# A new order table and a new choice of engines for the same operations: attention, a dense layer and a routed layer in one kernel

## The chip, the cores and the metric

The kernel runs on one core of one Trainium2 chip. The metric is the device time of one execution, in microseconds (us). The engines are named as in the profile: PE is TensorE (matmuls and transposes; PEld is its loading of weights), DVE is VectorE, ACT is ScalarE, POOL is GpSimd, SP is SyncE, which issues most DMAs.

## The reference, cut to what matters

```python
# attention: q, k, v are (2, 8, 768, 64); keys within 16 of the query, and 24 pooled blocks of 32
k_sum, v_sum = blocks of k (max) and of v (mean)
scores_l = where(|i - j| < 16, scale * q @ k.T, -1e9)
scores_s = scale * q @ k_sum.T + log(32)
a = softmax over both, with + 1e-09 in the divisor
x = (a @ [v, v_sum]) as 1536 tokens x 512
# dense layer (d_ff 768)
h = maximum(maximum(x @ w1, x @ w2), x @ w3);  x = h @ w_out
# routed layer: 8 experts, F = 1024
do_compute = x @ w_skip > 0;  logits = x @ w_gate;  e = argmax(logits);  g = its softmax weight
out = x;  out[do_compute] = x + g * (maximum(x @ w1[e], 0) @ w2[e])
```

## The kernel before, in words

**Stages.** The first stage is attention, for 4 groups of 384 tokens and 4 pairs of heads: scores (PE, L226 and L231), masked row maximum (DVE, L243), exponent (ACT, L250), divisor (DVE, L255 and L256), scaling (POOL, `norm`, L260), transposes (PE, L265) and their copies (L270), the product with the values (PE, L278). Its result is split into a high part and a low part (`xh` L286, `xl` L289), whose products are summed to keep fp32 accuracy. The dense layer's weights lie in memory as 64-bit words and are converted on the chip in steps (L305 to L330, on ACT, POOL and DVE), which also give a high and a low part. A chain (L337) is 12 matmuls of one group, one block of the hidden layer and one of the three weights; L344 (ACT) and L346 (DVE) take the maximum, L351 and L354 split the result, L364 multiplies by `w_out`, and L370 to L388 copy the sums out, from where DMAs write them to `out` and to `x2d`. A fold (L402 to L427) multiplies `w_out` with the gate and the skip weights, so that the logits come out of the same matmuls.

**Routing.** For each group `route` (L467 to L493) finds the experts, `rp` (PE, L509 to L512, with the counts L542) the place of each token among those of its expert, `rd` (`route3`, DVE, L521 to L531) the row, and three indirect DMAs on POOL (`rs`, L536) write token numbers and gate weights to `table`. The three of one group follow one another: each waits for the one ahead of it to land.

**The second layer.** It goes by pairs of tiles of 128 tokens of one expert. The tokens of a pair are gathered from `x2d` by the rows of `table` (`fetch`, POOL, L718, into `xn`), transposed (`turn_x`, PE, L705) and split into high and low (`put_x`, ACT L712 into `xth`, DVE L713 into `xtl`). In `pair`, first(f) (L1093) is 12 matmuls for one of 8 blocks of the hidden layer, second(f) (L1105) is 6. At f = 5 the transposes of the next pair stand in PE's queue, so they need the next pair's `xn` by then:

```python
first(0); first(1)
for f in range(8):
    if f == 5:
        turn_x()
    if f + 2 < 8:
        first(f + 2)
    if f == 5:
        next_x(t + 2)
    second(f)
```

 The weights of an expert come as 16 chunks `raw0` to `raw15` (L730), each split into a high part on ACT (`wh`, L736) and a low part on DVE (`wl`, L738). first(0) to first(3) need the chunks 0, 2, 4 and 6, first(4) to first(7) the chunks 1, 3, 5 and 7, second(f) the chunk 8 + f. The names `wl0_2`, `wl1_4` and so on are storage of first-layer weights that is used again.

**Order.** The work up to the first pair is 979 numbered operations. The list `ORDER` (L64 on) gives their numbers in the order in which they are emitted. Each engine works through its own instructions in that order and waits at the first whose inputs or buffers are not ready, so the list sets what stands behind what on each engine. The dictionary `HOME` (L53) names the engine of some operations by kind and index: `c4` (L326, the high part of a weight), `fv` (the copy of the extended values), `ph` (L286), `td` (L270); what is not named there goes to ACT. `w_cb` (L313), `h_low` (L354) and `norm` (L260) call POOL in the code and do not look into `HOME`.

Of the kernel before, what the change touches and what calls it, by code (L numbers as in the profile page):

```python
# [50 lines left out]
PORTED, SWITCH = 0.5, 0.06  # L51

HOME = {  # L53
# [4 lines left out]
}  # L58
HOME = {(n, i): e for (n, e), v in HOME.items() for i in v}

ORDER = [
# [46 lines left out]
]  # L108


# [1300 lines left out]
```

## Time and profile before

| | |
|---|---|
| time, median of 3 runs | 448.0 us (446.93 to 448.46) |
| the profiled execution's own time | 448.98 us |
| its span in the trace | 447.2 us |
| mean granted clock of PE | 0.996 |
| busy: PE, PEld | 432.3 us (97%), 389.2 us (87%) |
| busy: DVE, ACT, POOL | 233.1 us (52%), 184.3 us (41%), 138.1 us (31%) |
| start of the first matmul of the first pair (L1093) | 287.00 us |

A time in a row is counted from the span's start. A row of the timeline joins instructions of one kind that follow one another on one engine (xN of them); what stands in brackets is the time in which the engine was idle ahead of it, and what that wait ended with. An engine's busy share over the whole span says little here, since the stages differ; the windows give it by stretch.

### The profile page before, as it was taken

The numbers are of one execution on the slowest core, as the hardware profiler recorded it, in microseconds if no ns is written. First come the engines' busy times: TensorE is split into PE (matmuls) and PEld (weight loads), VectorE is DVE, ScalarE is ACT, GpSimd is POOL, SyncE is SP. The second block draws the span as 40 slices with busy tenths as digits, with TensorE's granted clock in tenths as the row PEclk, the third lists the DMA queues.
The fourth block names the chain that finished last, engine by engine and source line by source line (L and its number), as shares of the span: only waits on it lengthen the run. The fifth ranks groups of instructions, "written<-read, shape, count | busy, mean of one in ns | idle before, by whom it ended". The sixth has DMA issues, their size and how long they took to land.

```text
span 447.2 us, 9609 instructions
## 1 busy us (share of the span) xinstructions
PE 432.3 (97%) x3558; PEld 389.2 (87%) x3558; DVE 233.1 (52%) x738; ACT 184.3 (41%) x507; POOL 138.1 (31%) x191
## 2 busy tenths in 40 slices
PE   8999999999999999999999999799999999999995
PEld 3668889999789999998999999798989889798874
DVE  4899998989852531043214235868226651232321
ACT  3798984743685754107121037211114521212210
POOL 0666561434222522011601322131316034140400
PEclk9999999999999999999999999989999999999999
DMA  8987556456434512003042390242852193010111
GB/s 281 270 304 247 185 169 221 162 178 200 153 131 128 161 42 75 2 0 122 2 113 77 94 331 1 78 65 49 269 203 94 49 301 128 25 52 2 47 49 32
DMA packets 27584, 56.91 MB, mean 127 GB/s; under 512 B 6099, under 2 KB 8659, under 8 KB 27528
## 3 DMA queue, kind: packets, MB, share of 16 engines
q1 hardware_dynamic: 24968, 50.24, 35.3%
q0 software_dynamic: 2560, 5.96, 4.3%
q8 instruction: 30, 0.49, 0.5%
q14 instruction: 26, 0.21, 0.2%
HBM read 46.69 MB, written 10.47 MB: 128 GB/s over the span
## 4 chain that ended last, share of the span: by engine, by line
PE 83%; DVE 9%; ACT 3%; issue 2%; POOL 2%; DVEq 0%; ACTq 0%; POOLq 0%
PE pm L337 30%; PE ph L1093 13%; PE pm L1105 12%; PE pm L364 11%; PE ph L1186 2%; PE po L278 2%; DVE cx L318 2%; PE sc L226 2%; ACT pr L250 1%; PE pm L159 1%; PE pm L1158 1%; PE pt L265 1%; PE pm L1228 1%; DVE pr L243 1%; POOL pr L260 1%
## 5 line engine op out<-in xcount | busy, mean ns | idle before, releaser
L337 PE MATMUL pm<-xh,wh 128*128 128x384 f32 x288 | 65.2, 346 | 1.2 <-ACT t L344 0.7
L337 PE MATMUL pm<-xl,wh 128*128 128x384 f32 x288 | 62.2, 336 | 0.0
L337 PE MATMUL pm<-xh,wl 128*128 128x384 f32 x288 | 62.2, 335 | 0.0
L1096 ACT ACTIVATE hth<-ph 128x256 fp32r<-128x256 f32 x40 | 15.4, 384 | 91.4 <-PE ph L1093 84.8
L337 PEld LDWEIGHTS pm<-xh,wh 128*128 128x128 f32 x288 | 49.6, 188 | 3.5 <-ACT t L344 1.0
L337 PEld LDWEIGHTS pm<-xl,wh 128*128 128x128 f32 x288 | 51.1, 188 | 0.0
L337 PEld LDWEIGHTS pm<-xh,wl 128*128 128x128 f32 x288 | 51.1, 188 | 0.0
L1097 DVE SCALAR_TENSOR_TENSOR htl<-ph,hth 128x256 fp32r<-128x256 f32 x40 | 16.8, 422 | 56.3 <-ACT hth L1096 56.3
L346 DVE TENSOR_TENSOR t<-pm,t 128x384 f32<-128x384 f32 x48 | 26.1, 553 | 34.7 <-PE pm L337 34.5
L364 PE MATMUL pm<-wh,h 128*128 128x260 f32 (+1 forms) x288 | 43.5, 289 | 0.3 <-ACT x L386 0.3
L260 POOL TENSOR_TENSOR pr<-pr,se 128x360 f32<-128x360 f32 x32 | 27.0, 854 | 50.8 <-DVE se L256 33.1
L250 ACT ACTIVATE pr<-pr,mx 128x120 f32<-128x120 f32 x96 | 36.7, 386 | 12.5 <-DVE mx L243 12.3
L364 PEld LDWEIGHTS pm<-wh,h 128*128 128x128 f32 x288 | 38.2, 190 | 1.6 <-ACT x L386 0.5
L354 POOL TENSOR_TENSOR h<-t,h 128x384 fp32r<-128x384 f32 x24 | 25.3, 1069 | 32.5 <-ACT h L351 32.5
L1105 PE MATMUL pm<-wh,hth 128*128 128x512 f32 x80 | 31.9, 398 | 0.0
L1105 PE MATMUL pm<-wh,htl 128*128 128x512 f32 x80 | 31.6, 395 | 0.0
L1105 PE MATMUL pm<-wl,hth 128*128 128x512 f32 x80 | 31.3, 391 | 0.0
L718 POOL DMA_INDIRECT xn<-x2d,inx x14 | 14.9, 1063 | 48.6 <-DVE xm L1059 29.3
L243 DVE CUSTOM_DVE_ANT_0 pr<-sc,mask 128x120 f32<-128x120 f32 x96 | 21.1, 277 | 16.2 <-PE sc L226 14.1
L344 ACT COPY t<-pm 128x384 f32<-128x384 f32 x24 | 11.4, 478 | 39.9 <-PE pm L337 34.7
L1093 PE MATMUL ph<-xth,wl 128*128 128x256 f32 x160 | 26.2, 285 | 1.5 <-DVE wl L738 1.5
L1093 PE MATMUL ph<-xth,wh 128*128 128x256 f32 x160 | 26.6, 289 | 0.7 <-ACT xth L712 0.7
(337 smaller groups left out, 834.7 us busy)
## 6 DMA issues: line engine op xcount, KB each, us to landing
raw<-in_m SPq DMA_DIRECT2D x48, 256.0 KB, 5.0
raw<-in_wx SPq DMA_DIRECT2D x22, 512.0 KB, 4.3
vx<-in_vx SPq DMA_DIRECT2D x14, 288.0 KB, 3.5
qt<-in_qt SPq DMA_DIRECT2D x16, 192.0 KB, 4.1
raw<-in_vt SPq DMA_DIRECT2D x8, 384.0 KB, 5.9
x2d<-raw SPq DMA_DIRECT2D x12, 256.0 KB, 4.1
kx<-in_kx SPq DMA_DIRECT2D x8, 360.0 KB, 3.7
out<-raw SPq DMA_DIRECT2D x9, 256.0 KB, 3.2
```

The lines of the kernel that those rows point to most:

```text
L243: nc.vector.tensor_tensor_reduce(pr[:, t, :], sc[:, t, :], mask[:, mv, :], -0.125, 3.0e38, ALU.add, ALU.min, mx[:, t:t + 1])
L250: nc.scalar.activation(pr[:, t, :], pr[:, t, :], AF.Exp, bias=mx[:, t:t + 1], scale=-1.0, accum_out=se[:, h, t:t + 1])
L260: nc.gpsimd.tensor_tensor(pr, pr, ST["se", u, p][:, h].unsqueeze(2).broadcast_to([P, TPG, KT]), ALU.mult)
L337: nc.tensor.matmul(ST["ch", u, f, j], l[j, f][:, c * P:(c + 1) * P], r[u][:, c, :], start=(cs[0] == 0 and n == 0), stop=(cs[-1] == KC1 - 1 ...
L346: nc.vector.tensor_tensor(ST["t1", u, f], ps, ST["t1", u, f], ALU.max)
L354: nc.gpsimd.tensor_tensor(HL[u, f], ST["t1", u, f], HH[u, f].bitcast(F32), ALU.subtract)
L364: nc.tensor.matmul(ps, l[u, f][:, t * P:(t + 1) * P], r[3, f][:, lo:hi], start=(part != 1 and n == 0), stop=(part != 0 and n == len(ops) - 1))
L718: nc.gpsimd.indirect_dma_start(out=xn[t], out_offset=None, in_=x2d, in_offset=bass.IndirectOffsetOnAxis(ap=inx[:, t, 0:1], axis=0), bounds ...
L1093: nc.tensor.matmul(ps, w[:, o:o + P], r[:, d, :], start=(n == 0), stop=(n == 3 * KC1 - 1))
L1096: nc.scalar.activation(hh, ps, AF.Relu)
L1097: nc.vector.scalar_tensor_tensor(hl, ps, 0.0, hh.bitcast(F32), ALU.max, ALU.subtract)
L1105: nc.tensor.matmul(py[i], l[:, o:o + P], r, start=(f == 0 and n == 0), stop=(f == 7 and n == 2))
```

## The change

Only two tables differ. `HOME` names other indices: `c4` on POOL goes from 11 to 8 of them, `fv` on POOL from 3 to 6, `ph` on DVE from 4 to 6, `td` on DVE from 3 to 10; and it has entries for `nm`, `hl` and `cb` on DVE. `ORDER` is a new permutation of the same 979 numbers. All code behind the tables is the same and stands 6 lines further down, so L738 of before is L744 of after, L1093 is L1099.

```diff
 HOME = {
-    ("c4", "Pool"): [0, 1, 3, 6, 7, 8, 12, 19, 20, 22, 23],
-    ("fv", "Pool"): [(0, 0), (0, 1), (1, 2)],
-    ("ph", "DVE"): [(0, 0), (0, 2), (1, 1), (1, 2)],
-    ("td", "DVE"): [(0, 0, 1), (0, 2, 1), (1, 3, 1)],
+    ("c4", "Pool"): [0, 1, 2, 5, 6, 19, 20, 22],
+    ("cb", "DVE"): [6, 11],
+    ("fv", "Pool"): [(0, 1), (1, 2), (1, 3), (2, 0), (2, 3), (3, 0)],
+    ("hl", "DVE"): [(0, 0), (0, 2), (0, 3), (0, 4), (1, 0), (1, 1), (2, 0), (2, 3), (2, 4), (2, 5), (3, 0),
+        (3, 1), (3, 2), (3, 3), (3, 5)],
+    ("nm", "DVE"): [(0, 3, 0), (1, 1, 0), (1, 3, 0), (2, 0, 1), (2, 1, 0), (2, 2, 0), (2, 3, 0), (3, 0, 1),
+        (3, 1, 0), (3, 1, 1), (3, 2, 1), (3, 3, 0)],
+    ("ph", "DVE"): [(0, 0), (0, 2), (1, 1), (2, 1), (2, 2), (2, 3)],
+    ("td", "DVE"): [(0, 0, 0), (0, 1, 1), (2, 0, 0), (2, 0, 1), (2, 1, 0), (2, 2, 0), (3, 1, 0), (3, 2, 0),
+        (3, 2, 1), (3, 3, 0)],
 }
...
 ORDER = [
-    5, 25, 27, 6, 49, 26, 7, 0, 51, 50, 8, 28, 34, 52, 35, 9, 37, 36, 10, 73, 29, 11, 38, 12, 76, 58, 39,
...
```

**The end of the first layer on DVE.** `rw`, `rsl`, `rdo` and `rsi` belong to `rd` of the last group, `xm` is a copy of the gathered tokens, `xtl` the low part of the first pair's tokens, `wl` a low part of the second layer's weights. Before, DVE's queue at the end of the first layer reads:

```order
L1059 COPY xm0_3992<-xn0_3476 128x512
L521 TENSOR_TENSOR rw_3790<-pm_3870,con_103 128x24
L1059 COPY xm1_3993<-xn1_3477 128x512
L522 TENSOR_TENSOR rw_3790<-rw_3790,roh_3795 128x24
L524 TENSOR_REDUCE rsl_3890<-rw_3790 128x3
L525 TENSOR_SCALAR rdo_3797<-rdo_3797 128x3
L527 TENSOR_TENSOR rsi_3893<-rsl_3890,rdo_3797 128x3
L531 COPY rw_3790<-pm_3867 1x16
L738 TENSOR_TENSOR wl1_4_3762<-raw13_3465,wh1_4_3761 128x512
L713 TENSOR_TENSOR xtl_3481<-ptx0_3474,xth_3480 128x4x128
L713 TENSOR_TENSOR xtl_3481<-ptx1_3475,xth_3480 128x4x128
L738 TENSOR_TENSOR wl2_3_3727<-raw11_3463,wh2_3_3726 128x512
```

Behind these stand the low parts of the chunks 6, 3, 9 and 1, in this order, and then the first pair's own work. After, the same place reads:

```order
L744 TENSOR_TENSOR wl2_4_3795<-raw14_3465,wh2_4_3794 128x512
L1065 COPY xm0_3992<-xn0_3475 128x512
L1065 COPY xm1_3993<-xn1_3476 128x512
L719 TENSOR_TENSOR xtl_3480<-ptx0_3473,xth_3479 128x4x128
L719 TENSOR_TENSOR xtl_3480<-ptx1_3474,xth_3479 128x4x128
L527 TENSOR_TENSOR rw_3802<-pm_3884,con_103 128x24
L528 TENSOR_TENSOR rw_3802<-rw_3802,roh_3807 128x24
L530 TENSOR_REDUCE rsl_3900<-rw_3802 128x3
L531 TENSOR_SCALAR rdo_3809<-rdo_3809 128x3
L533 TENSOR_TENSOR rsi_3903<-rsl_3900,rdo_3809 128x3
L537 COPY rw_3802<-pm_3881 1x16
L744 TENSOR_TENSOR wl0_5_3798<-raw15_3466,wh0_5_3797 128x512
```

All low parts but that of chunk 15 now stand ahead of `xtl`, and `rd` of the last group has moved from ahead of `xtl` to behind it.

**The low parts that the first pair needs.** Ahead of the last group's `route`, where before had the low parts of the chunks 5, 7, 2, 8 and 4 between the copies of the logits (`lg`), DVE's queue after reads:

```order
L744 TENSOR_TENSOR wl1_1_3608<-raw4_3455,wh1_1_3607 128x512
L744 TENSOR_TENSOR wl1_2_3671<-raw7_3458,wh1_2_3670 128x512
L744 TENSOR_TENSOR wl2_2_3676<-raw8_3459,wh2_2_3675 128x512
L744 TENSOR_TENSOR wl1_0_3577<-raw1_3452,wh1_0_3576 128x512
L744 TENSOR_TENSOR wl2_0_3585<-raw2_3453,wh2_0_3584 128x512
L744 TENSOR_TENSOR wl1_3_3703<-raw10_3461,wh1_3_3702 128x512
L383 COPY lg_3761<-pm_3679 128x9
L744 TENSOR_TENSOR wl0_2_3653<-raw6_3457,wh0_2_3652 128x512
L383 COPY lg_3761<-pm_3706 128x9
```

The low part of chunk 6 has moved from behind `xtl` to ahead of the last group's routing.

**A fold on ACT.** L407 copies transposed `w_out` (`cr`) out of a PSUM buffer in the fold. L250 is the exponent of one tile of scores, three to a head (`pr0`, `pr1`). Before, ACT's queue at the third of the fold's six blocks reads:

```order
L250 ACTIVATE pr0_1719,se_1723<-pr0_1719,mx0_1720 128x120 x3
L407 COPY cr_1774<-pm_1738 128x512
L424 CAST wh3_4_1636<-pm_1728 128x10
L424 CAST wh3_3_1605<-pm_1699 128x10
L305 ACTIVATE cr_1778<-raw_1652 128x512
L250 ACTIVATE pr1_1721,se_1723<-pr1_1721,mx1_1722 128x120 x3
```

After:

```order
L256 ACTIVATE pr0_1711,se_1715<-pr0_1711,mx0_1712 128x120 x3
L430 CAST wh3_3_1568<-pm_1720 128x10
L430 CAST wh3_4_1589<-pm_1728 128x10
L256 ACTIVATE pr1_1713,se_1715<-pr1_1713,mx1_1714 128x120 x3
L413 COPY cr_1798<-pm_1739 128x512
L311 ACTIVATE cr_1805<-raw_1671 128x512
```

The copy has moved behind the exponents of the second head.

## Rows read from the trace of the kernel before

**Rows 1.** The page, part 1: busy time of each engine, share, instructions.

```profile
PE 432.3 (97%) x3558; PEld 389.2 (87%) x3558; DVE 233.1 (52%) x738; ACT 184.3 (41%) x507; POOL 138.1 (31%) x191
```

**Rows 2.** Windows: stretch, its length, busy PE, PEld, DVE, ACT, POOL; clock, DMA, GB/s.

```profile
30.00:40.00 10.00, 9.02 (x126) 7.38 (x124) 9.73 (x26) 9.35 (x25) 4.99 (x7) 1.00 0.76 233
...
200.00:272.00 72.00, 70.82 (x511) 68.49 (x510) 21.13 (x82) 21.43 (x56) 21.66 (x24) 1.00 0.37 115
272.00:290.00 18.00, 15.52 (x130) 14.69 (x130) 13.10 (x42) 8.74 (x20) 2.75 (x3) 0.99 0.10 36
```

**Rows 3.** Timeline, PE's waits up to the second layer: start, length, instruction, [idle before].

```profile
36.61 0.72 PE L226 MATMUL sc<-h,qt 64*64 64x96 f32 x24 [0.98 <-issue]
...
61.30 0.54 PE L265 MATMUL pt<-ident,pr 128*120 128x128 f32 x3 [0.65 <-POOL pr L260]
...
203.40 0.97 PE L337 MATMUL pm<-xh,wh 128*128 128x384 f32 x4 [0.72 <-ACT t L344]
...
232.76 0.99 PE L337 MATMUL pm<-xh,wh 128*128 128x384 f32 x4 [0.46 <-ACT raw L370]
...
280.26 1.00 PE L364 MATMUL pm<-wh,h 128*128 128x262 f32 x6 [0.25 <-ACT x L386]
```

**Rows 4.** Timeline at 118 us: a copy of the fold on ACT.

```profile
118.48 0.57 ACT L407 COPY cr<-pm 128x512 f32<-128x512 f32 x1
```

**Rows 5.** Timeline of the change to the second layer, 285 to 290 us.

```profile
286.40 0.15 DVE L531 COPY rw<-pm 1x16 f32<-1x16 f32 x1
286.48 0.67 DVE L738 TENSOR_TENSOR wl<-raw,wh 128x512 fp32r<-128x512 f32 x1
286.76 1.30 POOL L536 DMA_INDIRECT table<-rtab,rsi  x1 [1.28 <-DVE rw L531]
...
287.00 0.74 PE L1093 MATMUL ph<-xth,wh 128*128 128x256 f32 x4 [0.72 <-ACT xth L712]
287.08 1.27 DVE L713 TENSOR_TENSOR xtl<-ptx,xth 128x512 fp32r<-128x512 f32 x2
...
289.60 0.58 PE L1093 MATMUL ph<-xth,wl 128*128 128x256 f32 x1 [1.50 <-DVE wl L738]
```

**Rows 6.** Windows with the granted clock around that wait (columns as in rows 2).

```profile
289.00:290.00 1.00, 0.40 (x2) 0.40 (x3) 1.00 (x2) 0.00 (x0) 0.00 (x0) 0.78 1.00 359
291.00:292.00 1.00, 1.00 (x7) 1.00 (x6) 0.78 (x2) 0.39 (x1) 0.48 (x1) 0.50 0.62 35
293.00:294.00 1.00, 1.00 (x10) 1.00 (x10) 0.17 (x1) 0.38 (x1) 0.00 (x0) 1.00 0.94 334
```

**Rows 7.** The chain that ended last, 287 to 310 us: start, length, what.

```profile
289.60 5.19 PE ph L1093 x29
...
298.98 1.42 PE ph L1093 x12
```

**Rows 8.** POOL's timeline: the next two scatters and the gather that follows.

```profile
291.52 1.00 POOL L536 DMA_INDIRECT table<-rtab,rsi  x1 [3.46 <-DMA table<-rtab,rsi]
298.17 0.98 POOL L536 DMA_INDIRECT table<-rtab,rsi  x1 [5.64 <-DVE hq L624]
...
302.28 1.01 POOL L718 DMA_INDIRECT xn<-x2d,inx  x1 [0.31 <-issue]
```

**Rows 9.** From issue to landing: the scatter of 238.7 us.

```profile
DMA to landing us min/median/max: 3.7/3.7/3.7
```

**Rows 10.** From issue to landing: the scatter of 291.5 us.

```profile
DMA to landing us min/median/max: 6.4/6.4/6.4
```

**Rows 11.** From issue to landing: the gather of 302.3 us.

```profile
DMA to landing us min/median/max: 4.8/4.8/4.8
```

**Rows 12.** PE's timeline, 305 to 309 us: the transposes of the next pair.

```profile
307.24 1.03 PE L705 MATMUL ptx<-ident,xn 128*128 128x128 f32 x8
```

**Rows 13.** Lines by engine, POOL: count, busy, mean ns, idle before and what ended it.

```profile
L260 POOL TENSOR_TENSOR pr<-pr,se 128x360 f32<-128x360 f32 x32 | 27.0, 854 | 50.8 <-DVE se L256 33.1 <-DVE lg L377 12.1 <-DVE xl L289 1.9
L354 POOL TENSOR_TENSOR h<-t,h 128x384 fp32r<-128x384 f32 x24 | 25.3, 1069 | 32.5 <-ACT h L351 32.5
```

91 rows, old and new, of the table ORDER are left out of this document.

## The prediction

> **What bounds the kernel now.** I read the busy times first, then the windows, then PE's timeline for each wait, and last the change between the two layers closely. PE is the bound: 432.3 us busy, far above the other engines [rows 1]. The windows say where that does not hold. In 30 to 40 us DVE is busy 9.73 of 10 us and PE 9.02; in 200 to 272 us PE is busy 70.82 of 72; in 272 to 290 us PE is busy 15.52 of 18 [rows 2]. So the start-up goes at DVE's pace, then PE goes nearly without a break, and there is one large hole at the end of the first layer. The last scores for which PE still waits at length for the start-up begin at 36.61 us; behind them PE's waits up to the second layer are short ones [rows 3]. In the hole PE waits 0.72 us for the high part of the first pair's tokens, and 1.50 us for a low part of the weights [rows 5].
>
> The new table puts the same instructions on PE ahead of the scores of 36.61 us and the same ones behind them. So the change of the time is what these scores move by, plus what PE's later waits and its clock change by. That gives five terms.
>
> **A, the start-up.** These scores wait for DVE's masked row maximum, and the same set of DVE instructions stands ahead of it in both orders. Putting the rows of before through the new order by hand gives an end 0.2 us later: the engine that bounds has the same work, and only its gaps, 0.27 of 10 us there [rows 2], can move. The other engines' moves could lengthen or close such gaps over four such windows, so the bounds are -1.0 and +1.0. I take **+0.2**, the hand-worked end.
>
> **B, short waits in the middle.** Gone by the new order are the wait for ACT's copy at 203.40 (0.72; the copy stands behind an exponent of the routing, which waits for DVE), that at 232.76 (0.46), that at 280.26 (0.25) [rows 3], and a transpose that waited for POOL's `norm`, 0.65 at 61.30, of which I count 0.4. That is 1.8. New are two. In the fold ACT's copy, 0.57 long at 118.48 [rows 4], moves behind three exponents; the chain on PE that took the PSUM buffer freed by this copy now waits some 0.75 for it. One transpose of the third group stands some 0.5 ahead of its `norm`, by POOL's 0.854 for one [rows 13]. These are about 1.0, estimates from these rows. Net **-0.8**; bounds -1.8 (the new ones find cover) and +1.2 (the old ones return in other places and the new ones are 1.2 in all).
>
> **C, the change of layers.** Before, the low part of chunk 6 stands on DVE behind `rd` of the last group, the low part of chunk 13, both `xtl` and the low part of chunk 11. first(0) needs it, so PE stops for 1.50 us at 289.60, in its fourth matmul by `wl` [rows 5]. Behind that wait the granted clock fell: 0.78 in the window of 289, 0.50 in that of 291, 1.00 in that of 293 [rows 6]. The 36 matmuls of first(0) to first(2) end with the 5.19 us piece that starts at 289.60, at 294.79; begun at 287.00 they took 7.79 us, where twelve take 1.42 at the full clock [rows 5, 7]. Three times 1.42 is 4.26, with 0.1 for small gaps 4.4. In the new order chunk 6's low part, and all others but chunk 15's, are made ahead of `xtl`, and `xtl` stands ahead of `rd`. The wait and the fall of the clock behind it go: 7.79 - 4.4 = 3.4, and the first matmul starts about 0.15 earlier, since its transposes stand ahead of `rp` on PE. **C = -3.5.** What covers the moved low parts (the one of chunk 6 and some four more, 0.67 each [rows 5]) is DVE's idle time in 262 to 285: in the whole of 200 to 290 it is busy only 34 of 90 us [rows 2].
>
> **D, what is late next.** `rd` of the last group now stands on DVE behind `xm` and both `xtl`. Before, its last instruction begins at 286.40 and POOL's first scatter at 286.76; `xtl` ends at 287.08 + 1.27 = 288.35 [rows 5]. After, `xtl` ends at about 287.6 (the 0.67 of a low part no longer lies ahead of it), the six instructions of `rd` take until 288.55, and the first scatter begins at 288.75: 2.0 later. Three scatters in a row, then the gather of the second pair's tokens hang on this. Before: 286.76, 291.52, 298.17, the second gather at 302.28, which lands 4.8 after its issue, at 307.04 [rows 5, 8, 11]. PE reached the transposes of that pair at 307.24 [rows 12], so this chain had some 0.2 to 0.6 us to spare (the second half of the eight transposes, 0.5 later, uses the tile that lands last); I take 307.7 as the latest landing without a wait. With C, PE gets there at 307.24 - 3.5 = 303.7. So the time that C wins is waited out there unless the scatters come faster. How fast they come is the open size: one of before landed 3.7 after its issue with little other traffic [rows 9], the second of the last three 6.4 after [rows 10], beside the writes of the last results. With d as the shift of the landing, C + D = 307.04 + d - 307.7 or, with d rounded, -0.65 + d. If all gaps stay, d = +2.0, and a semaphore's 0.1 is added: +1.45. If both gaps shrink to 3.7 + 0.3, the third scatter begins at 288.75 + 8.0 = 296.75 rather than 298.17, d = -1.4, and C + D = -1.95. I take +0.5 for d, nearer to the rows of before with the last writes partly out by then: 288.75 + 5.7 + 4.25 = 298.7. **C + D = 0.0** (rounded up for the semaphore).
>
> **E, the clock again.** PE then stands idle for over 3 us at the transposes. Behind the 1.50 us wait of before the clock was at half from about 289.56 (a mean of 0.78 is half for 0.44 of that us) to 293, 3.4 us [rows 6], which costs half of it, 1.7. If it falls here, the same comes again; bounds 0 and 1.7. I take **+1.3**, since the idle time is longer than that which went ahead of the fall.
>
> The change of `HOME` moves copies between ACT, POOL and DVE, none of them a bound outside the start-up: nothing beyond A and B. Its entries for `nm`, `hl` and `cb` reach no instruction, so the 0.854 and 1.069 us instructions of POOL stay there [rows 13].
>
> **The sum.** 0.2 - 0.8 + 0.0 + 1.3 = +0.7 against the execution's own 448.98, so 449.7. That execution stands 0.98 above the median of 448.0, so the forecast is **448.7**. I use the median's scale below.
>
> A rule to weigh: the Trainium skill, "DMA: Bandwidth & Descriptors", section "Anatomy of one DMA", gives a DMA a fixed cost of about 2.0 us that is mostly the receipt of the write. By an estimate from it a scatter would be done about 3 us after POOL begins it. The rows above, 3.7 and 6.4, are longer, and the measured ones count; the rule would lead to the faster rival below.
>
> **The rivals.** *Slower: the scatters keep their gaps.* The writes of the last results follow the last group's sums, which don't move, so the second scatter can meet them as before; d = 2.0 and the clock falls in full: 0.2 - 0.8 + 1.45 + 1.7 = +2.5, 450.5. For it speaks the 6.4 [rows 10]; against it, that the first scatter begins 2.0 later, when more of these writes are out. It decides once d is over about 1.3. *Faster: the scatters come quiet.* d = -1.4 or less, and the idle time is too short for a fall of the clock: 0.2 - 0.8 - 2.0 = -2.6, 445.4. For it speaks the 3.7 [rows 9]. Against it: even then PE waits about 1.5 us at the transposes, as long as the wait that went ahead of the fall of before [rows 5]. *The change does not do what it says.* The order has its place for `norm`, the low parts of h and two clamps as if these ran on DVE, and they run on POOL, at 0.854 and 1.069 us [rows 13]. Consumers on PE then stand closer behind POOL than the order counts on; 0.65 at 61.30 [rows 3] is what one such wait is worth, and with 27 such places three or four more of them come to +2, 450.0. Against it speaks that POOL is busy only 31% [rows 1].
>
> **How the numbers follow.** About 0.3%, 1.34 us, can be told from no change. The forecast with its spread of A, B and d (447.3 to 449.9) has 0.47, of which 0.05 is slower by more than that; the slower rival 0.25, of which 0.02 ends within; the faster one 0.15; POOL 0.13, of which 0.02 within. Faster 0.15, same 0.46, slower 0.39. The range goes to the ends of the rivals with half a microsecond to a microsecond for A and B: 444.9 to 451.6.
>
> **What would show it.** In the profile after: the scores of 36.61 begin within 35.6 to 37.6 (A). No wait of 0.72 and 0.46 for ACT at the chains near 203 and 233, and one of some 0.7 at a chain near 119 that an ACT copy of the fold ends (B). The first matmul of the first pair at about 286.9 with no wait for `wl` behind it and a clock of 1.00 in 287 to 293 (C). The first scatter of the last group at about 288.75, the third at about 298.7, PE idle from about 304 to 307.5 ahead of the transposes, ended by the DMA of `xn` (D), and a clock of 0.5 right behind (E). If there is no wait at these transposes, D is wrong and the kernel is faster by some 3 us; if `wl` is still waited for, C is wrong.

## The result: slower by 1.5%, and the profile after

The changed kernel takes 454.46 us (median of 4 runs, 452.41 to 457.75) where the kernel before takes 448.23: a ratio of 1.0146, with an interval of 1.0116 to 1.0177. Measured once more beside other kernels (e5 below) it took 452.9 against 448.52, 1.0097 (1.0067 to 1.0127). It is slower by 4 to 6 us, and outside the predicted range of 444.9 to 451.6. Its runs also differ more among each other than those of before.

The profiled execution took 454.23 us, its span is 452.4 and the mean granted clock 0.988 (before 0.996). The page's first part, as [rows 1]:

```profile
PE 433.8 (96%) x3558; PEld 391.6 (87%) x3558; DVE 245.4 (54%) x747; ACT 180.3 (40%) x498; POOL 139.6 (31%) x191
```

The windows of [rows 2] now read:

```profile
30.00:40.00 10.00, 8.24 (x115) 6.43 (x114) 9.86 (x29) 8.73 (x24) 2.48 (x3) 0.92 0.78 243
200.00:272.00 72.00, 71.92 (x529) 70.19 (x519) 24.03 (x83) 19.62 (x49) 22.11 (x24) 1.00 0.34 115
272.00:290.00 18.00, 18.00 (x141) 17.83 (x139) 14.64 (x39) 8.30 (x19) 2.89 (x3) 1.00 0.04 16
```

In 200 to 290 us PE is busy all but 0.08 us: the holes that the prediction saw go have gone. The losses are elsewhere. These are PE's long waits in its timeline, one each in the start-up, the middle and the second layer, with the one ahead of the first pair (as [rows 3, 5, 12]):

```profile
36.41 0.73 PE L232 MATMUL sc<-h,qt 64*64 64x96 f32 x24 [1.76 <-issue]
...
161.18 1.51 PE L284 MATMUL po<-ps,vx 120*64 120x64 f32 x24 [2.34 <-POOL vx L220]
...
290.85 0.74 PE L1099 MATMUL ph<-xth,wh 128*128 128x256 f32 x4 [0.42 <-ACT xth L718]
...
310.17 1.29 PE L711 MATMUL ptx<-ident,xn 128*128 128x128 f32 x8 [2.22 <-DMA xn<-x2d,inx]
```

Behind each of the three long ones the granted clock falls to half (windows of 2 us, columns as in rows 2; the clock is the third number from the end):

```profile
38.00:40.00 2.00, 2.00 (x8) 2.00 (x9) 1.97 (x6) 1.82 (x5) 0.00 (x0) 0.60 0.50 141
40.00:42.00 2.00, 2.00 (x9) 2.00 (x8) 1.97 (x9) 1.60 (x5) 1.87 (x3) 0.55 0.52 201
160.00:162.00 2.00, 0.82 (x16) 0.82 (x18) 0.94 (x7) 0.00 (x0) 1.86 (x3) 0.82 0.00 0
162.00:164.00 2.00, 2.00 (x21) 1.88 (x18) 0.16 (x1) 0.75 (x2) 1.16 (x2) 0.50 0.20 36
164.00:166.00 2.00, 2.00 (x16) 2.00 (x15) 0.86 (x2) 1.51 (x3) 0.52 (x1) 0.83 0.81 262
310.00:312.00 2.00, 1.83 (x12) 1.62 (x13) 1.37 (x5) 0.00 (x0) 0.00 (x0) 0.86 0.11 43
312.00:314.00 2.00, 2.00 (x11) 2.00 (x10) 0.00 (x0) 0.03 (x1) 0.09 (x1) 0.50 0.07 1
314.00:316.00 2.00, 2.00 (x8) 1.59 (x8) 1.62 (x5) 1.32 (x3) 0.17 (x2) 0.78 0.07 1
```

A mean of 0.60 over 2 us is half the clock for 1.6 of them. Summed in this way each fall lasts 3.4 us, in which PE gets 1.7 us less of work done. Before had one such fall, behind the wait of [rows 5, 6]. Two more falls make 3.4 us of lost work; with the wait of 2.34 at 161 us that is 5.7, beside the 5.25 us by which the execution's own time rose (454.23 - 448.98). Not all of it reaches the end; the part on the prediction splits it.

What holds PE at 161 us is told by POOL's timeline there:

```profile
156.68 1.53 POOL L266 TENSOR_TENSOR pr<-pr,se 128x360 f32<-128x360 f32 x2 [4.61 <-DVE se L262]
158.17 2.08 POOL L360 TENSOR_TENSOR h<-t,h 128x384 fp32r<-128x384 f32 x2
160.31 0.82 POOL L220 COPY vx<-v 24x768 f32<-24x768 f32 x1
```

`pv` (PE, L284) of the last group's first pair needs `vx`, and the copy that completes it (`fv` 3 0, L220) is one of those that the new `HOME` puts on POOL. There it stands behind two norms, which wait for DVE's divisor and through it for ACT's exponents of another pair, and behind two low parts of h. PE was done with its last chain at 158.84 and stood idle until 161.18.

### The profile page after: what moved, and what is told of

It reads as the page before. It is cut to its first block, busy times and chain, and to the rows that moved or that the text cites. A ratio compares the mean times of both kernels' runs of the same rounds, so it can differ in the third digit from the quotient of the medians.

```text
span 452.4 us, 9616 instructions
## 1 busy us (share of the span) xinstructions
PE 433.8 (96%) x3558; PEld 391.6 (87%) x3558; DVE 245.4 (54%) x747; ACT 180.3 (40%) x498; POOL 139.6 (31%) x191
## 4 chain that ended last, share of the span: by engine, by line
PE 74%; DVE 9%; ACT 5%; POOL 4%; issue 4%; DMA 2%; POOLq 0%; ACTq 0%; DVEq 0%
PE pm L343 23%; PE pm L370 12%; PE ph L1099 12%; PE pm L1111 11%; PE ph L1192 2%; PE po L284 2%; ACT pr L256 2%; PE pt L271 2%; PE sc L232 2%; POOL h L360 2%; PE pm L165 2%; DMA raw<-in_wx 1%; DVE cx L328 1%; PE pm L1164 1%; DVE wl L336 1%
## 5 line engine op out<-in xcount | busy, mean ns | idle before, releaser
L319 POOL TENSOR_SCALAR cx<-cx 128x512 f32<-128x512 f32 x24 | 19.2, 804 | 35.6 <-ACT cx L315 30.0
L1099 PE MATMUL ph<-xth,wh 128*128 128x256 f32 x160 | 26.4, 288 | 0.4 <-ACT xth L718 0.4
L1099 PEld LDWEIGHTS ph<-xth,wh 128*128 128x128 f32 x160 | 23.3, 190 | 2.8 <-ACT xth L718 0.5
```

Of the source, the lines that this page charges most:

```text
L319: nc.gpsimd.tensor_scalar(x, x, HIGH, LOW, ALU.min, ALU.max)
L1099: nc.tensor.matmul(ps, w[:, o:o + P], r[:, d, :], start=(n == 0), stop=(n == 3 * KC1 - 1))
```

## The experiments

The medians stand beside the median of the kernel before in the same group of runs, since it moves between groups (448.1 to 449.0). An edit of `ORDER` is shown by the numbers that move; what they are stands behind it.

### The copy on POOL (e1)

In the changed kernel number 695 (`fv` 3 0) goes ahead of 550 and 553 (norms), 656 and 648 (low parts):

```diff
-... 655, 550, 553, 649, 756, 707, 656, 647, 643, 704, 648, 695, 610, ...
+... 655, 695, 550, 553, 649, 756, 707, 656, 647, 643, 704, 648, 610, ...
```

> The changed kernel with one operation moved in the order table: the copy of the extended values of the last group, first pair (fv 3 0, on POOL by the new HOME), stands ahead of two norms and two low parts of h on POOL instead of behind them. Theory 1 (PE's wait of 2.34 us at 161.18 for this copy, and the half clock of 161.3 to 164.7 behind it, are most of the loss): both go, 454.4 - 2.3 - 1.7 = about 450.4. Theory 2 (the wait only stands in for others just behind it, because the whole stretch is short of POOL and DVE): the norms or low parts now come 0.8 later and PE waits for those, 453.5 or more. Both leave the waits at the start-up and at the second pair's transposes.

Measured: 453.37 against 449.03, ratio 1.0085 (1.0055 to 1.0115). PE's timeline at the same matmul:

```profile
159.65 0.57 PE L284 MATMUL po<-ps,vx 120*64 120x64 f32 x12 [1.27 <-POOL h L360]
```

The wait shrinks from 2.34 to 1.27 and doesn't go. What is late now is another input of the same matmul, ACT's copy of the second head's transposes:

```profile
159.07 0.48 ACT L276 COPY ps<-pt 120x384 f32<-120x384 f32 x1
```

It ends at 159.55, behind a copy for a later pair (`fv` 3 2) and three high parts of h. In the changed kernel the same copy ends at 159.56, hidden behind POOL's at 161.13. The h that the row names as releaser is no input of this matmul. Theory 1's 450.4 did not come; theory 2 has the time about right, but what PE waited for is neither a norm nor a low part. Mending one feeder was not enough.

### HOME's unused entries (e2)

The changed kernel, with `norm`, `h_low` and `w_cb` looking into `HOME`:

```diff
-        nc.gpsimd.tensor_tensor(HL[u, f], ST["t1", u, f], HH[u, f].bitcast(F32), ALU.subtract)
+        eng = nc.vector if HOME.get(("hl", (u, f))) == "DVE" else nc.gpsimd
+        eng.tensor_tensor(HL[u, f], ST["t1", u, f], HH[u, f].bitcast(F32), ALU.subtract)
```

(the same in `norm` and `w_cb`).

> The changed kernel with the same two tables, but norm, h_low and w_cb look into HOME, so that 12 norms, 15 low parts of h and 2 clamps run on DVE. Theory 1 (the loss is where the order stands against engines that the code does not use): two of the four POOL instructions ahead of fv 3 0 go to DVE, the wait of 2.34 us shrinks to 0.5 or less and the half clock behind it goes: about 450.5, unless DVE pays for it. Theory 2 (DVE is the bound of the start-up, and three more norms there at over 0.5 us each lengthen it): the scores of 36.4 us begin 0.5 to 1.5 later, and the total is 451.5 to 453. If neither the wait nor the total moves, the entries are no part of the cause.

Measured: 453.71 against 449.03, ratio 1.0091 (1.0066 to 1.0116).

```profile
160.28 0.42 PE L285 MATMUL po<-ps,vx 120*64 120x64 f32 x7 [2.25 <-DVE xl L296]
```

POOL's copy ends sooner, but a low part of h on DVE, which waits for ACT, now stands ahead of the `xl` that frees the PSUM buffer `po`; the wait is 2.25 instead of 2.34. Neither the wait nor, clear of the noise, the total moved: running these entries on DVE does not give the loss back.

### route3 ahead of xtl (e3)

```diff
-... 921, 919, 922, 915, ...
+... 921, 922, 919, 915, ...
```

(919 is `put_x`, 922 `rd` of the last group.)

> The changed kernel with route3 of the last group back ahead of the first pair's low parts xtl on DVE; nothing else moves. Theory 1 (the transposes of the second pair wait for the last group's three scatters, which start 2 us later than they need): first scatter at about 1.2 to 2 us earlier against the first matmul of the pair, the wait of 2.22 us at 310.17 falls below 1, the half clock behind it goes: 454.4 - 1.5 - 1.7 = about 451.2. Theory 2 (the scatters' pace is set by the last results' writes, not by when the first one starts): the second gather lands at the same distance from the first matmul, the wait stays over 1.5 and the total stays within 1 us of 454.4.

Measured: 452.74 against 449.03, ratio 1.0085 (1.0055 to 1.0116). The first scatter begins 0.79 behind the first matmul of the pair, instead of 1.85. The transposes wait 1.42 instead of 2.22 (3.06 in e5), where theory 1 had under 1, and PE waits 0.62 for `xtl`:

```profile
292.23 0.38 PE L1099 MATMUL ph<-xtl,wh 128*128 128x256 f32 x1 [0.62 <-DVE xtl L719]
...
309.70 1.29 PE L711 MATMUL ptx<-ident,xn 128*128 128x128 f32 x8 [1.42 <-DMA xn<-x2d,inx]
```

No half clock follows here. But the transposes begin 19.30 us behind the pair's first matmul, as in the changed kernel (19.32); with the same end e4, e5 and e1 have 19.92, 20.18 and 20.62. So a sooner `rd` moves the first scatter by 1.06 us and may bring the tokens up to about 1 us sooner, which this run doesn't settle; part of the shorter wait is only that PE comes later, held up by `xtl`. The total is not clear of the changed kernel's either.

### The start-up of before (e4), and that of after alone (e13)

e4 takes the order and engines of before for the 169 operations up to the scores of 36.6 us, and the changed order for the rest; e13 the other way round.

> The order and the engines of the kernel before up to and with the scores of 36.6 us (169 of the 979 operations), and behind them the changed kernel's order. Theory 1 (the changed start-up ends no later, but leaves PE idle for 1.76 us in one piece at 34.65 to 36.41, and the clock falls to half at 38.3 to 41.6 behind it): the pieces of before come back, 0.97 and 0.98, no fall there, but of its 1.65 us some comes back as short waits of PE for POOL at 50 to 61 us: 452.8 to 453.9. Theory 2 (the fall there costs nothing, as DVE is the bound to 60 us anyway): 454.4 within 0.5.

> The changed kernel's order and engines up to and with the scores of 36.4 us, and behind them the order and engines of the kernel before. Theory 1 (the start-up is part of the loss only by the half clock that its one wait of 1.8 us can leave behind): most executions within 0.5 us of the kernel before, some 1 to 2 us slower at a granted clock 0.003 to 0.004 lower; median +0.2 to +0.8. Theory 2 (it is a loss by its waits too): span times clock is over 1 us above that of the kernel before, median +1.2 or more. Theory 3 (no part of it): within 0.2 of before and no lower clock.

Measured: e4 452.32 against 449.03, 1.0075 (1.0046 to 1.0103), its six runs all at a clock of 0.994 or 0.995 and within 1.0 us, where the changed kernel's clocks lie between 0.983 and 0.997. e13 448.99 against 448.33, 1.0022 (1.0003 to 1.0042); four of its twelve runs lie at a clock of 0.990 to 0.992 and above 450, the others mostly where before lies. e4 lies below its theory 1 (452.8 to 453.9) and is not clear of the changed kernel (1.0097 in e5); e13 is as its theory 1 says. Together they fit this: the wait in one piece (1.76 in the changed kernel, 0.99 in e4, 0.98 in [rows 3]) costs little by itself, since the scores begin no later for it (36.41 and 36.61). It leaves the clock at half behind it in some executions only. In the profiled executions with this start-up and a wait of 1.60 to 1.85 the clock fell in two of nine, both with a wait of 1.76; the six longer waits were followed by none. That the four slow runs of e13 had this fall is read from their mean clock; the one that was profiled had none.

### The end alone, and later transposes (e5 to e9)

e5 is the changed kernel again. e6 has the order and engines of before up to the opening of the second layer's buffers, then the changed order. e7, e8 and e9 are e6, the changed kernel and the kernel before with one edit in `pair`:

```diff
-            if f == 5:
+            if f == 6:
                 turn_x()
             if f + 2 < 8:
                 first(f + 2)
-            if f == 5:
+            if f == 6:
                 next_x(t + 2)
```

> The changed kernel as it is, beside the three that follow, since its runs differ more among each other (452.4 to 457.8) than those of before, with the granted clock between 0.983 and 0.994. Theory 1: the time follows the number of times that the clock falls to half behind PE's three long waits, which differs from run to run; span less (1 - clock) x span stays within 446.5 to 448.5. Theory 2: the runs differ in waits, and that number spreads as widely as the time.

> The order and engines of the kernel before up to the opening of the second layer's buffers (868 of the 979 operations), behind it the changed kernel's order: only the end of the first layer is changed. Theory 1 (the end by itself is worth nothing: the 1.5 us wait for the low part of chunk 6 and the half clock behind it go, and the same time is waited out at the second pair's transposes, at 20 us behind the first matmul, with the half clock behind that): 448.3 to 450.5, PE idle 2.2 to 3.5 us ahead of the transposes. Theory 2 (the end is part of the loss: the scatters 2 us later cost more than the early low parts give): 451 or more. Theory 3 (the end is a gain that the middle has eaten): 446.5 or less.

> The same as the kernel with only the end changed, and the transposes of the next pair and the splitting that follows them stand at f = 6 instead of f = 5, so 2.8 us of matmuls later in PE's queue, in every pair. Theory 1 (the gain at the end of the first layer is waited out at the transposes): the wait there falls to under 0.7 us, the clock stays at 1.00, and the gain comes through: 449.0 - 3.5 = 445.0 to 446.5. Theory 2 (what is late at the transposes is late for something else just behind): 448 or more.

> The changed kernel with the transposes of the next pair at f = 6 instead of f = 5 in every pair; nothing else moves. Theory 1: the wait of 2.22 us and the half clock behind it (1.7) go, the middle's losses stay: 450 to 451.5. Theory 2 (the later splitting holds up the first matmuls of each following pair): within 1 us of the changed kernel, with a new wait at the first matmul of a pair.

> The kernel before with the transposes of the next pair at f = 6 instead of f = 5; no table changed. Theory 1 (there is no wait at these transposes before, so a later place gives nothing; the 446.4 of the kernel with the changed end and this edit needs both): within 0.7 us of the kernel before. Theory 2 (the later place is a gain by itself): 447.5 or less.

| kernel | median | before beside it | ratio (interval) |
|---|---|---|---|
| e5 changed kernel | 452.90 | 448.52 | 1.0097 (1.0067 to 1.0127) |
| e6 end only | 450.98 | 448.52 | 1.0045 (1.0018 to 1.0072) |
| e7 end only, f = 6 | 446.44 | 448.52 | 0.9957 (0.9940 to 0.9974) |
| e8 changed, f = 6 | 450.81 | 448.52 | 1.0059 (1.0031 to 1.0086) |
| e9 before, f = 6 | 449.26 | 448.13 | 1.0020 (0.9997 to 1.0042) |

The changed end alone is slower than before, between its theories 1 (450.5 at most) and 2 (451 or more); with later transposes it is faster, and these alone bring nothing. On the changed kernel (e8 against e5) the median falls by 2.1 us, as expected, though the two intervals still overlap. e6's profiled execution, 452.41, is the slowest of its six. PE gets to the transposes at 304.28 there and waits:

```profile
307.90 1.97 PE L706 MATMUL ptx<-ident,xn 128*128 128x128 f32 x8 [3.62 <-DMA xn<-x2d,inx]
```

and the clock falls while it waits and for long behind it:

```profile
306.00:308.00 2.00, 0.10 (x1) 0.10 (x2) 1.35 (x5) 0.00 (x0) 0.00 (x0) 0.79 0.54 213
308.00:310.00 2.00, 2.00 (x10) 2.00 (x11) 0.00 (x0) 0.00 (x0) 0.06 (x1) 0.50 0.07 1
310.00:312.00 2.00, 2.00 (x11) 2.00 (x11) 0.00 (x0) 0.00 (x0) 0.13 (x1) 0.50 0.07 1
312.00:314.00 2.00, 2.00 (x8) 1.61 (x7) 1.11 (x4) 1.35 (x3) 0.00 (x0) 0.50 0.66 200
```

Six us at half clock cost about 3 here, and the wait ate the rest of what the early low parts gave. In e7 the same transposes wait 0.75, the clock stays:

```profile
309.13 1.28 PE L706 MATMUL ptx<-ident,xn 128*128 128x128 f32 x8 [0.75 <-DMA xn<-x2d,inx]
```

Of e5's theories neither is right as it stands: span less what the clock costs lies at 446.9 to 449.1 over eight runs, so 2.2 us of the 5.85 us of spread stay without it. Most of it is the clock.

### The feeders of one matmul (e10, e11), and all three mended (e14)

e10 is e8 with three things moved: `fv` 3 0 as in e1; the two copies of the transposes (704, 707) right behind these on ACT; and `fv` 3 2 (735), for a pair that needs it only at 234 us, out of their way behind `pv` 3 0 (708):

```diff
-... 645, 735, 640, 609, 642, 549, 655, 550, 553, 649, 756, 707, 656, 647, 643, 704, 648, 695, 610, ... 708, 711, ...
+... 645, 707, 704, 640, 609, 642, 549, 655, 695, 550, 553, 649, 756, 656, 647, 643, 648, 610, ... 708, 735, 711, ...
```

> The changed kernel with the transposes at f = 6 (which gave 450.8), and the three things that the values product of the last group's first pair (pv 3 0, PE, 161 us) waits for made sooner: fv 3 0 ahead of two norms and two low parts on POOL, the two copies td 3 0 right behind their transposes on ACT, and fv 3 2 behind pv 3 0. Theory 1 (PE has no other ready work at that point, since the last chain of the second group is done and the product with w_out needs all low parts of h, which POOL makes one after another until 163): pv 3 0 starts at once, but PE then waits over 1 us for POOL's low parts at the product with w_out, and the total is within 1 us of 450.8. Theory 2 (only these three were late): no wait of over 0.7 us from 155 to 170, 450.8 - 2.3 - 0.9 (the half clock, in some executions) = about 447.6.

> The same as the kernel with the sooner feeders, and the low parts of h of the second group that HOME names for DVE (1 0 and 1 1) run there, behind pl 2 3. Theory 1 (POOL's row of low parts is what limits the stretch): the wait at the product with w_out goes below 0.7 us, no half clock at 161 to 165, total 447.3 to 449. Theory 2 (PE's ready work is short by more than these two): a wait of over 1 us stays in 155 to 170 us, for DVE or ACT, and the total stays over 449.5.

> The changed kernel with all three causes mended: the start-up of before, the sooner feeders of the values product at 161 us, and the transposes at f = 6. Theory 1 (these three are the whole loss, and the changed end is a gain once the transposes don't wait): 446.2 to 447.3, at or a little below the 447.6 with the start-up left as changed. Theory 2 (something else in the changed middle still costs): 448 or more.

Measured: e10 447.64 against 448.13, ratio 0.9996 (0.9978 to 1.0013), so about 2.8 us less than e8 when each is held against its own before. PE's timeline in e10:

```profile
158.73 0.92 PE L284 MATMUL po<-ps,vx 120*64 120x64 f32 x24
...
162.60 0.75 PE L370 MATMUL pm<-wh,h 128*128 128x262 f32 x4 [0.72 <-POOL h L360]
```

`pv` 3 0 starts without a wait. Of the 2.34 us 0.72 comes back behind it, as a wait for POOL's low parts, and no half clock follows. From the start of `pv` 3 0 to the pair's first matmul it is 129.06 us here and 128.12 in e5, which had the wait and no fall: 0.9 of the 2.34 has come back by then. Theory 2 holds: one matmul had two late inputs, on two engines, and a copy for a later pair stood in the way of one of them. e11 moves two of POOL's low parts to DVE, with a low part `xl` (610) ahead of them, and is not better (448.65 against 448.13, 1.0014, 0.9995 to 1.0033): PE then waits 1.33 at 161.53, for DVE. e14, with the start-up of before, the feeders and f = 6 in the changed order, takes 446.31 against 448.33, 0.9948 (0.9929 to 0.9968). With these three mended the changed order is faster than the kernel before, and no other loss shows. e7, with the middle of before, is as fast (0.9957), so a gain from the changed middle doesn't show either.

### One more wait of before (e12)

e7 with the routing of the second group (682) moved behind 774, so that ACT's copy for the chain at 203 us no longer stands behind the routing's exponent:

```diff
-... 682, ... 774, ...
+... 774, 682, ...
```

> The kernel with only the end changed and the transposes at f = 6 (446.4), with the routing of the second group moved behind two maximum steps of the third group, so that the ACT copy which PE waits for at 203 us no longer stands behind the routing's exponent. Theory 1 (that wait of 0.72 us is on the path): it goes and the total falls by 0.5 to 0.8, to 445.7. Theory 2 (the time is waited out later, at the copies of 232 or 260 us): within 0.3 of 446.4.

Measured: 446.07 against 448.13, ratio 0.9951 (0.9930 to 0.9971). The wait of 0.72 is gone from PE's timeline there. The total is 0.4 below e7's, but before lies 0.4 lower in that group too, so whether it came through is not settled. e12 and e14 are the best kernels of the study, each 0.5% faster than the one before.

## Why the prediction was wrong

**What bounds the kernel** was read rightly: PE, with DVE in the start-up. The five terms, against the profiled executions:

- **A, the start-up.** Forecast +0.2, bounds -1.0 to +1.0; the scores begin at 36.41 instead of 36.61, so -0.2. The step that was missing is that the form of a wait counts too: PE got there sooner, waited 1.76 in one piece, and the clock fell. By e13 that is worth +0.66 in the median, in some executions about 2.
- **B, the middle: the step that failed.** From these scores to the first matmul of the pair it is 254.44 us (36.41 to 290.85) where before needs 250.39: +4.05, where B with the 0.15 of C had -0.95. The waits of 203.40, 232.76 and 280.26 went as forecast. That of 61.30 did not (0.56 at 61.46). The new wait that was forecast in the fold is 0.20 instead of 0.75 (at 121.29, and for DVE); one of 0.79 stands behind a later copy of the fold, at 126.64. The other, at a transpose of the third group, did not come. The two new waits that the term names add up to 1.25 and not to the 1.0 that it counts.

  But the sentence "the change of `HOME` moves copies between ACT, POOL and DVE, none of them a bound outside the start-up: nothing beyond A and B" was false. It argued from shares (POOL busy 31%) where an engine's order decides: a copy of 0.82 us on an engine that is two thirds idle ended PE's wait of 2.34 us, because what stood ahead of it waited for DVE and ACT. It is not all of the wait. PE was done at 158.84, and ACT's copy of the transposes, which the new `ORDER` puts behind other work, ends at 159.56: without POOL's copy PE would still have waited, some 0.7 here and 1.27 in e1. B names no such wait either. (`fv` 3 0 back on ACT, with the order as changed, was not run.)

  The second thing that failed is that no term stood for a fall of the clock ahead of 290 us. e5 is the same kernel with the same waits and no fall there:

```profile
36.52 0.73 PE L232 MATMUL sc<-h,qt 64*64 64x96 f32 x24 [1.82 <-issue]
160.15 0.92 PE L284 MATMUL po<-ps,vx 120*64 120x64 f32 x24 [2.34 <-POOL vx L220]
288.27 0.74 PE L1099 MATMUL ph<-xth,wh 128*128 128x256 f32 x4 [0.42 <-ACT xth L718]
```

  From the scores to the pair it needs 251.75, so the two falls are worth 2.7 of the +4.05, less than 1.7 each: behind the start-up PE gets to the transposes of 61 us only 0.8 later by the fall (25.05 behind the scores, 24.24 in e5), since it then waits less for POOL there; behind 161 us it is 1.6 (129.67 and 128.12). The other +1.36 lies 2.3 above the forecast of -0.95, which is about the wait of 2.34. This split is good to about 1 us: e9, with the order of before up to the pair, needs 251.35 for this stretch.
- **C, the change of layers.** As forecast: no wait for the low part, no fall of the clock from 166 to 310 us, a wait of 0.42 ahead of the first matmul (before 0.72).
- **D, what is late next.** As forecast in its place and its releaser; the wait is 2.22 here and 3.06 in e5, where over 3 was forecast. POOL's timeline after (as [rows 5, 8]):

```profile
292.70 1.30 POOL L542 DMA_INDIRECT table<-rtab,rsi  x1 [3.02 <-DVE rw L537]
299.22 1.00 POOL L542 DMA_INDIRECT table<-rtab,rsi  x1 [5.21 <-DMA table<-rtab,rsi]
303.30 0.98 POOL L542 DMA_INDIRECT table<-rtab,rsi  x1 [3.08 <-DVE p_fs L658]
305.97 1.06 POOL L724 DMA_INDIRECT xn<-x2d,inx  x1 [0.27 <-POOL inx L1114]
307.33 1.01 POOL L724 DMA_INDIRECT xn<-x2d,inx  x1 [0.31 <-issue]
```

  Against the first matmul the first scatter is at +1.85 (before -0.24), so 2.1 later, where 2.0 was forecast. From the first matmul to the transposes it is 19.32 us here, 20.18 in e5 and 20.73 in e6, where before needs 20.24. Measured from the first matmul, C + D was taken as about +0.15 and is -0.9 to +0.5. It came out near with parts of it wrong, and that is luck: the two gaps between scatters are 6.52 and 4.08 here (7.16 and 4.22 in e6), in sum 10.60 (11.38) where before has 11.41 and the forecast took 9.95; the slow scatter is now the first of the three, before it was the second [rows 10]. What made up for it here are the gathers of the two tiles, which land 4.2 and 3.4 us after their issue; the second took 4.8 in [rows 11], and the forecast kept that. These are the two of the changed kernel:

```profile
DMA to landing us min/median/max: 4.2/4.2/4.2
DMA to landing us min/median/max: 3.4/3.4/3.4
```

  The transposes begin as the first of them lands (305.97 + 4.2 = 310.17).

  By the Trainium skill, "DMA: Bandwidth & Descriptors", section "Anatomy of one DMA", a scatter would be done about 3 us after POOL begins it, an estimate. The three here landed after 6.2, 3.8 and 3.7, so the trace does not agree, and the faster rival that this rule led to did not come.
- **E, the clock behind the transposes.** Forecast +1.3; half the clock for 3.4 us, 1.7, in the profiled execution, and about 3 in e6.

From the first matmul to PE's last it is 155.41 us (290.85 to 446.26) where before needs 154.59 (287.00 to 441.59): +0.8, where C, D and E without the 0.15 had about +1.4. Some 0.5 more lies behind PE's last matmul (6.1 us to the end of the span, before 5.6). So the miss lies in B: in the wait of 2.34, and in the falls of the clock ahead of 290 us, for which no term stood. Of the rivals, the slower one (450.5) is about what the end alone gives (e6, 450.98 against 448.52). The one on `HOME`'s unused entries named the right engine, POOL, and the right consumer of its time, PE, but for another reason: by e2 running these entries on DVE does not give the loss back.

## What to carry to other kernels

When an operation changes its engine, look at what stands ahead of it in the new engine's queue and what that waits for; the engine's busy share says nothing about it. If a matmul waits, list all its inputs and its buffer with the times at which they are ready: moving one won 1.07 of the 2.34 us of wait, mending all of them some 1.4. And work that is made ready sooner is a gain only if the next thing in the same queue is ready too: the early low parts cost 0.45% until the transposes were moved 2.8 us down PE's queue, and gave 0.43% from then on.

## What the runs showed of the hardware

The same wait in the same kernel is followed by half the clock in one execution and not in another, and by the sum over the eight runs above most of the kernel's spread comes from that (2.2 of 5.85 us stay without it). In the profiled executions PE's waits of 2.25 to 2.34 us at the values product were followed by a fall in the changed kernel, e3 and e8 and by none in e2, e4 and e5. The wait of 1.50 us for the low part was followed by one in the kernel before and by none in e9 and e13 (1.51 and 1.53). All six waits at the transposes of 2.2 us and more (the changed kernel, e1, e2, e4, e5, e6) were followed by one, and those of up to 1.42 us there (e3, e7, e8) by none. A fall lasted 3.4 us in the three of the changed kernel, and about 6.8 in e6, where it began before PE was at work again. The length of the wait alone does not decide it: in the start-up waits of 1.82 to 1.85 were followed by none and two of 1.76 by one. So a wait of PE that is near these lengths has a price that is drawn anew in each execution, and a forecast for it needs a chance and not one value.
